# The denominators' matmuls join the visit in which keys meet values

## The chip, the cores and the metric

The kernel runs on one core of one Trainium2 chip. The metric is the time in microseconds (us) of one execution on the device. A core has a TensorE for matmuls (PE in the profile, its weight loads PEld), VectorE (DVE), ScalarE (ACT), GpSimdE (POOL), and SyncE (SP), which here only issues transfers. Matmuls write into PSUM, which has eight banks of 512 float32 columns on 128 partitions.

## The reference: linear attention, then a feed-forward layer

```python
proj = x @ w_phi                                   # per head, 64 -> 128
proj = proj - max(abs(proj), axis=-1)
phi(x) = concat([exp(proj), exp(-proj)])           # 256 features
kv  = einsum('bhsf,bhsd->bhfd', phi(k), v)
z   = sum(phi(k), axis=2)
num = einsum('bhsf,bhfd->bhsd', phi(q), kv)
den = einsum('bhsf,bhf->bhs', phi(q), z) + 1e-06
x   = (num / den) as [4608 tokens, 512]
h = x @ w_in;  e = exp(h - max(h));  solu = h * e / sum(e)
out = layernorm(solu) * g_ln @ w_out               # 512 -> 1024 -> 512
```

There are 8 batches with 8 heads of 576 tokens and 64 columns each. The 64 heads are worked through as 32 pairs of heads, and the feed-forward layer as 36 tiles of 128 tokens.

## The kernel before, in words

**Units and pairs.** A unit `u` (0 to 15) is one half of a batch: two pairs of heads, `sub` 0 and 1. Pair `n = 2u + sub`. For keys, a token tile of 256 or 128 columns is loaded (`rawk`), split into a high and a low part (`xh` on ACT, `xl` on POOL), projected (`pjk` on PE), reduced to its largest magnitude (`m`, DVE), shifted (`dk`, DVE) and put through exp twice (`ek`, ACT). Queries go `rawq`, `hq` (ACT, then POOL), `pq` (PE, four pieces of 288 tokens), `blk` (DVE transposes), a maximum over the features that passes PE twice (`mtp`, `mcp`) with DVE, POOL and ACT between, POOL subtracts, DVE transposes back (`pT`) and ACT makes the features `fq`. The first three units use other, plainer paths (`pjq`, `dT`).

**The visit.** For each pair, one function `visit` holds the PE in a tiled mode: the array is used as two halves of 64 columns, or as four strips of 32 columns, and several small matmuls run side by side. From pair 6 on (`JOIN`) the visit of pair n first makes the numerators of pair n-1 (`num`, two banks of 288 tokens, 64-column halves), then keys times values of pair n (`kvT`, 64-column halves), then the sums over the keys (`kvT<-zacc`, 32-column strips), in columns 256 to 383 of the same bank.

**The denominators.** `q_den` makes those of pair n-1: for two halves of 288 tokens, four matmuls on four 32-column strips, each half into a bank of its own (`den`). It is an operation of its own in the order: it may stand right behind the visit, or anywhere after it. ACT copies each half out (`dE`, `q_oe`). SP stores the rows to DRAM, loads them compactly (`cmp`), DVE takes the reciprocal (`cmr`), SP stores and broadcasts it (`rb`), and POOL multiplies it into the numerators (`xa`, `xb`).

**Keys-values on their way to the next visit.** DVE transposes the 384 columns of the visit's bank (`kvs`, `kv_turn`), SP stores them (`dk`), and four loads of 32 partitions each bring them back in the layout that the next visit's `num` and `den` take as weights (`kvf<-dk`, `kv_in`). Every SP transfer uses one of eight semaphores in turn.

**The feed-forward tile.** `h` (24 matmuls of 512 columns), maximum on DVE (`nm`), exp on ACT and product on DVE (`eu`), eight transposes on PE (`uT`), split on ACT and DVE (`uh`, `ul`), `o` (24 matmuls of 512 columns), scaling on ACT (`os`), store.

**PSUM.** Three banks are shared by all attention tiles (tag `a`: `pjk`, `pq`, `mtp`, `mcp`, `num`, `den`), one is the visit's alone (tag `kv`), `h` takes two, and two serve `uT` and `o` (tag `mo`).

**What sets the order.** `Plan.order` places every operation: it keeps a cost for each, latencies between engines, and a count of free buffers per tag; an operation is placed when its inputs and all its buffers are there, and among the ready ones priority decides. The priorities are the sums of two tables of numbers, `BASE` and `OFFSET`. The result is one fixed instruction order on each engine. At run time an engine works through its order and waits on semaphores at single instructions, so that a tile's bank is waited for at its first write, and not earlier.

```python
TILED = dict(visit=(1, 2), q_num=(1, 1), q_den=(2, 2))
PSUM_BUFS = dict(a=3, kv=1, h=1, mo=2)
```

Of the kernel before, what the change touches and what calls it, by code (L numbers as in the profile page):

```python
# [20 lines left out]
P = 128  # L21
KCOL = 2 * S
HC = S // 2
# [3 lines left out]
TILED = dict(visit=(1, 2), q_num=(1, 1), q_den=(2, 2))  # L27
K_PLAIN = (0, 1, 2)
# [19 lines left out]
PSUM_BUFS = dict(a=3, kv=1, h=1, mo=2)  # L48
# [19 lines left out]
)  # L68
OFFSET = (
# [289 lines left out]
def linear_attention_then_moe(ctx: ExitStack, tc, qT, qT2, kT, v, w_phi, w_in, g_ln, w_out, out):  # L359
# [22 lines left out]
    def bank(tag, shape, name):  # L382
        pool = psa if tag in ("a", "kv", "th", "tmo") else ps
        return pool.tile(shape, F32, tag=place(tag), bufs=1, name=name)
# [266 lines left out]
    def visit(st, sub, before):  # L651

        if before:
            q_num(*before)
        kv = st["kv", sub] = bank("kv", [P, 512], "kvT")
        for g in PARTS[sub]:
            e = st["kf", g]
            rv = st["rv", g] if g != 2 else st["vz"][:, sub : sub + 1]
# [645 lines left out]
```

## Time and profile before

| | |
|---|---|
| three runs | median 790.03 us (788.88 to 792.82) |
| the profiled execution's own time | 790.95 us |
| its span, first to last instruction | 789.2 us |
| mean granted TensorE clock | 0.994 |
| PE busy | 756.7 us |
| POOL, DVE, ACT busy | 470.9, 486.4, 405.8 us |

The profile is read as follows. A row of a group of instructions gives how often it ran, its busy time, the mean time of one in ns, and behind the second bar the idle time of its engine just before, with what ended it. A row of the timeline gives the start in us, the length, the engine, and what was made. A float32 matmul of this program is shown as two MATMUL instructions, a float32r one as one. The length of a matmul in the timeline is longer than its place in the stream, since matmuls overlap: the place is read from start to start.

### The profile page before, as it was taken

How to read it: one execution, taken by the hardware profiler on the slowest of the kernel's cores; microseconds unless marked ns; L12 is line 12 of the kernel's file. 1: busy time of each engine (PE TensorE's matmuls, PEld its weight loads, DVE VectorE, ACT ScalarE, POOL GpSimd, SP SyncE). 2: the span in 40 equal slices, each digit the busy share in tenths (PEclk: the TensorE clock that was granted, in tenths of full speed). 3: DMA queues.
4: the chain of work that ended last, by engine and by line, in shares of the span. 5: the costliest groups of instructions: out<-in, count | busy, mean ns of one | idle time of the engine just before them, and what ended most of it. 6: DMA issues, size and time to landing. Idle time of an engine off the chain costs nothing.

```text
span 789.2 us, 13661 instructions
## 1 busy us (share of the span) xinstructions
PE 756.7 (96%) x4935; PEld 562.2 (71%) x4935; DVE 486.4 (62%) x829; ACT 405.8 (51%) x814; POOL 470.9 (60%) x507
## 2 busy tenths in 40 slices
PE   5899898999999999999999999999999999999997
PEld 3565586767677777767776777777777776788886
DVE  4978684756675675756566686665756683444343
ACT  3876764564645565454745465463644655322322
POOL 1224897778687678585676759675776855231210
PEclk8999999999999999999999999999999999999999
DMA  6954442443526153442435343333334212200000
GB/s 203 374 122 122 104 103 52 108 110 104 119 73 135 53 123 104 106 100 70 125 81 121 85 108 100 90 88 92 87 99 114 78 43 78 52 28 14 27 28 27
DMA packets 105251, 75.96 MB, mean 96 GB/s; under 512 B 65376, under 2 KB 91488, under 8 KB 104672
## 3 DMA queue, kind: packets, MB, share of 16 engines
q1 hardware_dynamic: 105184, 75.10, 35.9%
q8 instruction: 39, 0.64, 0.4%
q14 instruction: 28, 0.23, 0.1%
HBM read 59.67 MB, written 15.38 MB: 95 GB/s over the span
## 4 chain that ended last, share of the span: by engine, by line
PE 72%; DMA 10%; DVE 5%; ACT 3%; POOL 3%; issue 3%; SPq 3%; ACTq 0%; POOLq 0%; DVEq 0%
PE o L347 21%; PE h L347 20%; PE kvT L347 9%; PE num L347 6%; PE pjk L347 5%; PE uT L347 3%; PE pq L347 3%; DMA rawq<-in_q 3%; PE den L347 3%; SPq L347 3%; DMA cmp<-d 2%; POOL hq L347 2%; DMA dk<-kvs 1%; PE pjq L347 1%; DMA rawk<-in_k 1%
## 5 line engine op out<-in xcount | busy, mean ns | idle before, releaser
L347 PE MATMUL o<-w_out_h,uh 128*128 128x512 f32 x288 | 116.0, 403 | 0.4 <-ACT uh L347 0.4
L347 ACT ACTIVATE ek<-dk 128x512 f32<-128x512 f32 (+1 forms) x160 | 87.2, 584 | 53.6 <-DVE dk L347 49.7
L347 PE MATMUL o<-w_out_h,ul 128*128 128x512 f32 x288 | 114.2, 397 | 0.0
L347 PE MATMUL o<-w_out_l,uh 128*128 128x512 f32 x288 | 113.9, 396 | 0.0
L347 POOL TENSOR_TENSOR zacc<-zacc,ek 128x512 f32<-128x512 f32 (+1 forms) x78 | 100.7, 1290 | 12.8 <-ACT ek L347 8.1
L347 POOL TENSOR_TENSOR hq<-rawq,hq 64x1152 fp32r<-64x1152 f32 x26 | 69.5, 2674 | 47.7 <-ACT hq L347 43.9
L347 PE MATMUL h<-win_h,mxh 128*128 128x512 f32 x288 | 93.6, 406 | 1.0 <-DVE eu L347 1.0
L347 PE MATMUL h<-win_h,mxl 128*128 128x512 f32 x288 | 90.8, 396 | 0.0
L347 PE MATMUL h<-win_l,mxh 128*128 128x512 f32 x288 | 90.6, 396 | 0.0
L347 DVE TENSOR_TENSOR ul<-uT,uh 128x512 fp32r<-128x512 f32 x72 | 48.2, 679 | 54.0 <-ACT uh L347 54.0
L347 ACT ACTIVATE fq<-pT 128x576 f32<-128x576 f32 x104 | 68.6, 688 | 17.3 <-DVE pT L347 14.0
L347 ACT CAST uh<-uT 128x512 fp32r<-128x512 f32 x72 | 41.6, 590 | 61.9 <-PE uT L347 48.8
L347 PE MATMUL num<-fq,kvf 128*64 128x288 f32 x512 | 69.2, 412 | 2.8 <-ACT win_h L347 1.8
L347 ACT ACTIVATE eu<-h,nm 128x1024 f32<-128x1024 f32 x36 | 40.3, 1118 | 57.6 <-DVE nm L347 57.5
L347 DVE TENSOR_REDUCE nm<-h 128x1 f32<-128x1024 f32 x36 | 43.8, 1218 | 41.7 <-PE h L347 41.6
L347 POOL TENSOR_TENSOR blk<-blk,mcol 128x1152 f32<-128x1152 f32 x26 | 55.6, 2137 | 17.2 <-ACT mcol L347 17.1
L347 PE MATMUL kvT<-ek,rawv 128*64 128x256 f32 x512 | 65.3, 387 | 0.0
L347 DVE STREAM_TRANSPOSE blk<-pq 128x288 f32<-128x288 f32 x104 | 46.5, 460 | 28.4 <-PE pq L347 22.8
L347 DVE TENSOR_TENSOR eu<-h,eu 128x1024 f32<-128x1024 f32 x36 | 43.9, 1220 | 32.4 <-ACT eu L347 32.4
L347 PEld LDWEIGHTS o<-w_out_h,ul 128*128 128x128 f32 x288 | 54.2, 188 | 13.6 <-DVE ul L347 0.4
L347 PEld LDWEIGHTS h<-win_h,mxl 128*128 128x128 f32 x288 | 54.2, 189 | 13.1 <-POOL mxl L347 0.2
L347 PEld LDWEIGHTS h<-win_l,mxh 128*128 128x128 f32 x288 | 54.1, 188 | 13.1
(107 smaller groups left out, 1584.1 us busy)
## 6 DMA issues: line engine op xcount, KB each, us to landing
rawq<-in_q SPq DMA_DIRECT2D x52, 288.0 KB
rb<-d SPq DMA_DIRECT2D x64, 144.0 KB
out<-os SPq DMA_DIRECT2D x36, 256.0 KB
rawk<-in_k SPq DMA_DIRECT2D x64, 128.0 KB
rawv<-in_v SPq DMA_DIRECT2D x64, 128.0 KB
dk<-kvs SPq DMA_DIRECT2D x28, 192.0 KB
kvf<-dk SPq DMA_DIRECT2D x112, 48.0 KB
wraw<-in_w_in SPq DMA_DIRECT2D x4, 1024.0 KB
```

The lines of the kernel that those rows point to most:

```text
L347: return self.tc.keep_in_program_order(method(*args, **kwargs))
```

## The change

The denominators of pair n-1 become part of the visit of pair n, for pairs 6 to 31. A new function, `q_den_joined`, is called at the visit's end, behind the sums over the keys. It splits the 576 tokens into 288, 224 and 64 (`DEN`): the first two share one bank of 512 columns, the last 64 tokens go to columns 384 to 447 of the visit's own bank. The copies follow (`den_oe`): one of 512 columns, one of 64 columns. `q_den` stays for the pairs that are not joined. The visit's bank comes from the shared group now, which has four banks; the operation `V` takes all four (two numerators, keys-values, denominators) when it is placed. The planner lets the transposition `kve` start before the denominators' part of the visit has ended. The two priority tables are replaced throughout.

```diff
+DEN = (288, 224, 64)
...
-PSUM_BUFS = dict(a=3, kv=1, h=1, mo=2)
+PSUM_BUFS = dict(a=4, h=1, mo=2)
...
-    -200.2, -1092.1, -271.3, 82.4, 164.5, 214.3, 259.1, 297.6, 340.8, 386.9, 433.6, 479.2, 529.5, 576.1, 626.1,
...
+    -465.0, -1432.2, -565.0, -22.2, 124.8, 203.9, 251.6, 298.6, 351.4, 395.4, 441.9, 492.3, 543.1, 595.6, 646.1,
...
-        kv = st["kv", sub] = bank("kv", [P, 512], "kvT")
+        kv = st["kv", sub] = bank("a", [P, 512], "kvT")
...
+        if before:
+            q_den_joined(*before, kv)
...
+    def q_den_joined(st, sub, kv):
+
+        po = st["den", sub, 0] = bank("a", [P, 512], "den")
+        st["den", sub, 1] = kv
+        for i, (out, c, c0) in enumerate(
+            ((po[:, :HC], 0, 0), (po[:, HC:512], 1, 0), (kv[:, 3 * F : 3 * F + D], 1, 512 - HC))
+        ):
+            n = DEN[i]
+            for s in range(2):
+                for j in range(2):
+                    r = slice(32 * (2 * s + j), 32 * (2 * s + j) + 32)
+                    nc.tensor.matmul(
+                        out[r], lhsT=st["kvf", sub][:, 2, r], rhs=st["qf", sub, c][:, j, s, c0 : c0 + n],
+                        start=i < 2, stop=True, skip_group_check=True,
+                    )
+
+    def den_oe(st, sub, c):
+
+        if c == 0:
+            st["dens", sub] = sb("dE", [P, S], name="dE")
+            nc.scalar.copy(out=st["dens", sub][:, :512], in_=st["den", sub, 0])
+        else:
+            nc.scalar.copy(out=st["dens", sub][:, 512:], in_=st["den", sub, 1][:, 3 * F : 3 * F + D])
...
-                alloc += [("a", ("abs", (pu, "num", ps_, c))) for c in range(2)]
-                early = {(pu, "qv", ps_, c, "num"): cost + (1 - c) * 2 * mm32(HC) for c in range(2)}
-                cost += 4 * mm32(HC)
+                num = [("a", ("abs", (pu, "num", ps_, c))) for c in range(2)]
+                alloc = num + alloc + [("a", ("abs", (pu, "den", ps_, 0)))]
+                den = sum(mm32(n) for n in DEN)
+                early = {(pu, "qv", ps_, c, "num"): den + cost + (1 - c) * 2 * mm32(HC) for c in range(2)}
+                early[u, "kve", sub] = den
+                cost += 4 * mm32(HC) + den
```

On PE, in the middle of the program before, a pair's denominators stand alone between feed-forward matmuls (`o`) and the next pair's query projections (`pq`); at the end of the name stands the size of what one matmul writes.

```order
L347 MATMUL o<-w_out_h,ul 128x512
L347 MATMUL den<-fq,kvf 32x288 x8
L347 MATMUL pq<-hq,w_hh 128x288
L347 MATMUL pq<-hq,w_l_84 128x288
L347 MATMUL pq<-hq,w_hh 128x288
L347 MATMUL pq<-hq,w_l_84 128x288
L347 MATMUL o<-w_out_h,uh 128x512
```

The pair's visit lies further up there, and the eight tiled matmuls of `den` have whole-array matmuls on both sides.

On PE of the changed program, one visit in the middle, with what stands ahead of it and behind it.

```order
L349 MATMUL o<-w_out_h,ul 128x512
L349 MATMUL num<-fq,kvf 64x288 x8
L349 MATMUL kvT<-ek,rawv 64x256 x8
L349 MATMUL kvT<-ek,vz_94 64x256 x2
L349 MATMUL kvT<-zacc,ones 32x128 x4
L349 MATMUL den<-fq,kvf 32x288 x4
L349 MATMUL den<-fq,kvf 32x224 x4
L349 MATMUL kvT<-fq,kvf 32x64 x4
L349 MATMUL uT<-ident,eu 128x128 x4
L349 MATMUL mtp<-ident,m_5107 36x128
L349 MATMUL pjk<-wph_h,xh 128x256
```

Numerators, keys-values, key sums and denominators are now one stretch. Counted over the whole program, PE enters a tiled stretch 53 times before and 38 times now. Of the denominators of the 26 joined pairs, 15 stood alone before and 11 stood right behind a visit.

On ACT of the changed program, the copies behind such a visit, with the semaphores on which each waits (PE_49, DVE_49, Pool_49 are those of the engines, DMAHW those of transfers).

```order
L349 COPY E<-num 128x288 [waits PE_49]
L349 CAST mxh<-xa 128x512
L349 COPY E<-num 128x288 [waits PE_49]
L349 COPY dE<-den 128x512 [waits DMAHW6_49,PE_49]
L349 ACTIVATE fq<-pT 128x2x288 [waits DVE_49,PE_49]
L349 ACTIVATE fq<-pT 128x2x288
L349 CAST xh<-rawk 128x128 [waits DMAHW5_49,PE_49,Pool_49]
L349 COPY dE<-kvT 128x64 [waits DVE_49]
```

The second copy of the denominators, of 64 columns, waits for DVE, and what DVE has to have done is the transposition of the same bank (`kvs<-kvT`). This holds in 22 of the 26 joined visits; in the other four, the transposition waits for the copy. The transposition waits for the last of the denominators' matmuls into its bank.

On SP of the changed program, the transfers behind one visit in the middle.

```order
L349 DMA dk<-kvs 128x384
L349 DMA vz_92<-in_v 64x128 x2
L349 DMA rawv<-in_v 128x256
L349 DMA d_4922<-dE 4x576
L349 DMA rawv<-in_v 128x256
L349 DMA kvf<-dk 32x12x32 x3
L349 DMA cmp<-d_4922 128x2x9
L349 DMA rawk<-in_k 128x128
L349 DMA rawk<-in_k 128x256
L349 DMA rawq<-in_q 64x1152 x2
L349 DMA kvf<-dk 32x12x32
L349 DMA rawq<-in_q 64x1152 x2
```

The fourth load of `kvf` stands behind the next pair's key and query loads; in the program before, the four loads stand together in 25 of 28 cases, and now in 15 of 28.

More of the change, by code (lines that the diff above doesn't have):

```diff
@@ L382, in bank @@
     def bank(tag, shape, name):
-        pool = psa if tag in ("a", "kv", "th", "tmo") else ps
+        pool = psa if tag in ("a", "th", "tmo") else ps
         return pool.tile(shape, F32, tag=place(tag), bufs=1, name=name)
@@ L1001, in linear_attention_then_moe @@
             tiles = [("e", g) for g in PARTS[sub]] + [("rv", g) for g in PARTS[sub]]
-            alloc, early = [("kv", ("kv", sub))], {}
+            alloc, early = [("a", ("kv", sub))], {}
             if u not in Z_PE:
@@ L1094, in linear_attention_then_moe @@
             joined = JOIN <= n + 1 < 4 * B
-            source = {"num": ("abs", ((n + 1) // 2, "V", (n + 1) % 2)) if joined else ("qo", sub), "den": ("qd", sub)}
+            visitor = ("abs", ((n + 1) // 2, "V", (n + 1) % 2))
+            source = {"num": visitor if joined else ("qo", sub), "den": visitor if joined else ("qd", sub)}
             if not joined:
@@ L1099, in linear_attention_then_moe @@
                     {(u, "qv", sub, 0, "num"): 2 * mm32(HC)})
-            add(("qd", sub), "tensor", 2 * mm32(HC), z + 5.5, q_den, (sub,), feat + [source["num"]],
-                [("a", ("den", sub, c)) for c in range(2)], fk, {(u, "qv", sub, 0, "den"): mm32(HC)})
+                add(("qd", sub), "tensor", 2 * mm32(HC), z + 5.5, q_den, (sub,), feat + [source["num"]],
+                    [("a", ("den", sub, c)) for c in range(2)], fk, {(u, "qv", sub, 0, "den"): mm32(HC)})
             for c in range(2):
                 for k, t in (("num", "E"), ("den", "dE")):
-                    add(("qv", sub, c, k), "scalar", act(HC, True), z + 5.1 + c, q_oe, (sub, c, k),
+                    own = (k, sub, c)
+                    fn, args, cols = q_oe, (sub, c, k), HC
+                    if joined and k == "den":
+                        fn, args, cols = den_oe, (sub, c), (512, D)[c]
+                        own = ("abs", ((n + 1) // 2, "kv", (n + 1) % 2)) if c else own
+                    add(("qv", sub, c, k), "scalar", act(cols, True), z + 5.1 + c, fn, args,
                         [source[k]] + ([("qv", sub, 0, k)] if c else []),
-                        () if c else [(t, (t, sub))], [(k, sub, c), (t, sub)])
+                        () if c else [(t, (t, sub))], [own, (t, sub)])
             add(("dr", sub), "sync", dma(16 * S), z + 6.4, den_rows, (sub,),
```

105 rows, old and new, of tables (BASE, OFFSET) are left out of this document.

## The prediction

> **What bounds the kernel now.** I read the page first: span, busy time by engine, granted clock.
>
> ```profile
> span 789.2 us, 13661 instructions
> PE 756.7 (96%) x4935; PEld 562.2 (71%) x4935; DVE 486.4 (62%) x829; ACT 405.8 (51%) x814; POOL 470.9 (60%) x507
> PEclk8999999999999999999999999999999999999999
> ```
>
> PE is busy for 756.7 of 789.2 us at the full clock; the next engine has 486.4. The windows view divides this into the start, the middle with the pairs of heads, and the end where only feed-forward tiles are left. Its columns are window, length, busy time and instructions of PE, PEld, DVE, ACT and POOL, granted clock, DMA share, GB/s.
>
> ```profile
> 0.00:100.00 100.00, 83.64 (x720) 55.57 (x721) 71.97 (x106) 66.27 (x139) 39.40 (x38) 0.95 0.61 183
> 100.00:680.00 580.00, 568.07 (x3727) 422.52 (x3729) 368.67 (x660) 309.75 (x625) 410.50 (x424) 1.00 0.38 94
> 680.00:789.20 109.20, 104.95 (x496) 84.13 (x488) 45.77 (x64) 29.79 (x52) 21.01 (x46) 1.00 0.08 27
> ```
>
> In the 580 us in which the joined pairs run, PE is idle for 11.9 us. So two things can be won there: matmul stream time, and those idle microseconds. The view of PE's waits in that window names them (us in total, times, longest).
>
> ```profile
> PE uT L347 <- DVE eu L347: 2.1, 1, 2.1
> PE pjk L347 <- ACT dE L347: 2.1, 2, 1.6
> PE mtp L347 <- DVE m L347: 1.4, 1, 1.4
> PE pq L347 <- DVE dk L347: 1.3, 1, 1.3
> PE h L347 <- DVE eu L347: 1.0, 1, 1.0
> PE num L347 <- DMA kvf<-dk: 0.9, 1, 0.9
> PE pq L347 <- POOL hq L347: 0.5, 1, 0.5
> PE den L347 <- ACT E L347: 0.5, 1, 0.5
> ```
>
> These eight are 9.8 us. No wait recurs at every pair: each is a single place where the order was tight.
>
> **The change part by part.** *A: fewer tiled stretches.* What a stretch of denominators costs alone and behind a visit is read from start to start in the timeline of PE (start, length, what). First a place with whole-array matmuls only, then one with denominators between such matmuls.
>
> ```profile
> 303.19 0.39 PE L347 MATMUL o<-w_out_h,ul 128*128 128x512 f32 x1
> ...
> 303.55 0.29 PE L347 MATMUL pq<-hq,w_l 128*128 128x288 f32 x1
> ...
> 328.66 0.39 PE L347 MATMUL o<-w_out_h,ul 128*128 128x512 f32 x1
> 328.99 1.18 PE L347 MATMUL den<-fq,kvf 128*32 128x288 f32 x16
> ...
> 330.33 0.29 PE L347 MATMUL pq<-hq,w_l 128*128 128x288 f32 x1
> ```
>
> From the `o` row to the second `pq` row it is 0.36 us without and 1.67 us with denominators: 1.31 us alone. Then the end of a visit, without and with denominators behind the key sums.
>
> ```profile
> 361.61 0.42 PE L347 MATMUL kvT<-zacc,ones 128*32 128x128 f32 x8
> ...
> 362.09 0.60 PE L347 MATMUL uT<-ident,eu 128*128 128x128 f32 x4
> 389.28 0.43 PE L347 MATMUL kvT<-zacc,ones 128*32 128x128 f32 x8
> ...
> 390.73 0.60 PE L347 MATMUL uT<-ident,eu 128*128 128x128 f32 x4
> ```
>
> From the key sums to `uT`: 0.48 and 1.45 us, so 0.97 us joined. A pair that moves saves 1.31 − 0.97 = 0.34 us. By the order, 15 of the 26 pairs stood alone; the other 11 already stand behind their visit and save nothing. **A = −15 × 0.34 = −5.1 us.** Bounds: if what is paid around a lone stretch is paid elsewhere, 0; if all 26 gained, −8.8.
>
> *B: three groups in place of two.* The columns stay 576. Joined, 288 columns take 0.97/2 = 0.49 us, so 64 take 0.11 us. What the third group adds is weight loads, shown by the tile's own row (shortest, median, longest in ns).
>
> ```profile
> L347 PEld LDWEIGHTS den<-fq,kvf x512: 106/110/110, 34.1 to 680.3; 128*32 128x32 f32 x171
> ```
>
> A load is 0.110 us, and each strip of the third group has two (`j` 0 and 1) with little streaming to hide under. Both fully hidden cost nothing more; both in full view cost 0.22 us where 0.11 us of columns were paid, so +0.11. I take +0.08 a pair, nearer the upper end, because a group this short hides less than a long one. **B = 26 × 0.08 = +2.1 us**, bounds 0 to +2.9. The Trainium skill ("TensorE: Matmul & The Clock Gate", LDWEIGHTS) puts a weight load at its columns over 1.2 in ns, an estimate of 27 ns for 32 columns; by that B would be about 0 and the sum 2.1 us lower. The row's 110 ns does not agree with it, and decides.
>
> *C: banks and copies.* Four banks are shared where three were, and one pair's denominators take one of them and not two. These rows price what holds a bank.
>
> ```profile
> L347 ACT COPY dE<-den 128x288 f32<-128x288 f32 x64 | 25.3, 401 | 13.1 <-PE den L347 12.2
> L347 ACT COPY mcol<-mcp 128x36 f32<-128x36 f32 x26 | 4.8, 184 | 23.1 <-PE mcp L347 23.1
> L347 ACT CAST mxh<-xa 128x512 fp32r<-128x512 f32 x20 | 12.3, 619 | 1.7 <-DMA out<-os 1.6
> L347 ACT ACTIVATE fq<-pT 128x576 f32<-128x576 f32 x104 | 68.6, 688 | 17.3 <-DVE pT L347 14.0 <-PE kvT L347 3.3
> L347 DVE STREAM_TRANSPOSE kvs<-kvT 128x384 f32<-128x384 f32 x28 | 16.0, 570 | 39.5 <-PE kvT L347 39.2
> ```
>
> ACT's two copies were 2 × 0.40 us. Now they have 512 and 64 columns: near 0.6 us (the cast of 512) and, between the 36 columns' 0.18 and the 288's 0.40, 0.21 us. That is the same ACT time, and ACT is at 51%. The waits on ACT go: `pjk` behind `dE`, 2.1 us, and `den` behind `E`, 0.5 us. Matmuls between two places of the order are priced by pitches from start to start (0.235 us for 512 columns, in E's rows). So counted, the bank that the first two groups fill next comes back to a matmul at least 1.5 us of matmuls later; it needs the 0.6 us copy and two handovers, so it is covered. The visit's own bank needs more: last denominators, `kvs` on DVE (0.57), the 64-column copy (0.21), three handovers, and its next writer is about 5 us of matmuls away in most pairs (1.9 us in one). **C = −2.6 us.** Bounds: −2.6, and upwards a new wait at every pair if a `fq` (0.69 us) runs ahead of the copies: 0.6 + 0.69 + handovers of about 0.4 is 1.7 against the 1.5, so 26 × 0.2 = +5.2. What queues behind the 64-column copy on ACT while it waits for DVE is `fq` and `uh`, on which the next visit and `o` depend; in its row `fq` waits 14.0 us in all for DVE and none for ACT's own order. The Trainium skill ("PSUM — Partial Sum Buffer", Terms) says that two engines on one bank and quadrant at once collide, reads included; that fits copy and transposition taking turns, and no run here shows a collision.
>
> *D: the new order elsewhere.* The priorities are all new, so each wait of the list above may go and others come. Two were traced through the new order. `uT` behind `eu`, 2.1 us: it arose where 2.9 us of matmuls lay between the last `h` and `uT`, so 5.0 us were needed; now at least 5.5 lie there. `mtp` behind `m`, 1.4 us: less than 3.3 us of matmuls lay between `pq` and `mtp` in 10 of 26 pairs, now in one. **D = −3.5 us.** Bounds: all other waits of the list too except those of C, −7.2; or as many new ones of the same size as the two removed, about +4.
>
> *E: keys-values on their way.* The transposition waits for the last denominators' matmul into its bank, so this path starts 0.97 us later in the 26 pairs, whatever the planner lets start early. The chain of waits shows it where it decides, at the last pair (start, length, what), with one query load and the pitch of `h` from the timeline.
>
> ```profile
> 667.49 2.56 PE kvT L347 x28
> 670.07 0.59 DVE kvs L347
> 670.68 1.85 DMA dk<-kvs
> ...
> 674.58 0.57 SPq L347
> ...
> 675.19 2.30 DMA kvf<-dk
> ...
> 677.63 2.16 PE num L347 x16
> ```
>
> ```profile
> 672.40 0.63 PE L347 MATMUL h<-win_h,mxh 128*128 128x512 f32 x2
> 672.87 0.63 PE L347 MATMUL h<-win_l,mxh 128*128 128x512 f32 x2
> 160.64 5.46 DMA rawq<-in_q
> ```
>
> The path takes 677.63 − 670.05 = 7.58 us; 6.7 us of matmuls covered it and 0.9 us was waited. Now the denominators stand ahead of its start, and 24 matmuls of `h` at 0.47/2 us and the change of mode, 5.9 us, remain: 1.7 us waited, **+0.8 us**. At the other pairs a median of 16 us of matmuls covers the path. But the fourth `kvf` load has moved behind query loads in nine pairs, and in four of these it stands so late in the joint order of all engines that 0.3 to 0.4 us of matmuls are left before `num`. SP runs ahead of that order when its waits are met, so it mostly goes out earlier; I take one SP issue (0.6 us) lost at each of the four, **+2.4 us, E = +3.2 us**. Bounds: +0.8, and each of the four waiting for its whole transfer, 2.30 + 0.14 − 0.35 = 2.1 us, so +9.2.
>
> *The start and the end.* Before pair 6 nothing is joined. By the order 66 us of matmuls stand ahead of the first `h`, 73 before, but PE is idle for 16.4 us of the first 100, and its DMA share of 0.61 there is the highest of the three: the loads bound it and have not moved, so 0, bounds ±2. The last tiles repeat their pattern.
>
> **Sum:** −5.1 + 2.1 − 2.6 − 3.5 + 3.2 = −5.9 us, made against the span of 789.2 us: 783.3. The profiled execution took 790.95, 0.9 above the runs' median, so I carry the difference to the median: 790.03 − 5.9 = **784.1 us**.
>
> **The rivals.** *More falls away:* the four-bank group takes all the middle's listed waits but the one at the last pair (8.9 of 9.8) and the late loads go out early (E = 0.8): −5.1 + 2.1 − 8.9 + 0.8 = −11.1, about 779; with all 26 joined at the best price (A −8.8) 775.2. For it: no wait recurs, so a better order can remove each. Against it: an order this full makes new single waits.
>
> *The gain is swallowed:* the copies behind each visit are late by the 0.2 us of C's upper bound. −5.9 + 5.2 = −0.7, about **789.3**. For it: two copies, a transposition and `fq` now compete behind the same last matmul, where one bank could be emptied while the other was filled. Against it: ACT's share of 51%, and the 5 us before the visit's bank is written again. The Trainium skill ("TensorEngine Tiling (Array Packing)", PSUM Bottleneck) warns that tiling speeds up TensorE and not the emptying of PSUM; it would come out here as this rival, and before the change the 12.2 us in `dE`'s row are ACT waiting for PE, not the reverse.
>
> *Slower:* the fourth `kvf` load, behind two 288 KB query loads, is held until the first of these has landed: 5.46 − 2 × 0.6 = 4.2 us after its own issue. At the four places that is 4.2 + 0.14 − 0.35 = 4.0 us each, 16.0, and at the five others, with some 3 us or more left, up to 1.3 us each. With the four alone, −5.9 − 2.4 + 16.0 = +7.7: **797.7 us**. It decides once these loads cost above 2.4 + 5.9 = 8.3 us, 2.1 us at each of the four. For it: their place in the order; the one wait for `kvf` seen was real. Against it: SP has slack, and its order is not a timetable.
>
> *Not what it says:* the planner's early start for the transposition has no counterpart in the order's waits; that is in E. The visit itself is joined in all 26, so this rival has no case of its own.
>
> **How the numbers follow.** The forecast 784.1 has a chance of 0.50, its own range 780 to 788; more falling away 0.13; swallowed 0.22; slower 0.15. A measurement of this kernel can tell about 0.5% from no change, that is 786.1 to 794.0. Faster: four fifths of the forecast (0.40), the 0.13 and little of the swallowed case (0.02): 0.55. Slower: most of the slower case (0.13) and a little of the swallowed one (0.02): 0.15. Same: 0.30. The range goes from 775.5, close to the best case, to 796, a little short of the slower one.
>
> **What the changed profile would show.** A and B: no `den` between whole-array matmuls in pairs 6 to 31, and about 0.97 + 0.08 = 1.05 us from the key sums to the next whole-array matmul beyond its 0.48; 1.3 or more there would undo A. C: no PE wait on `dE` above 0.3 us; a row of many small ones on `dE` or `kvs` is the swallowed case. D: `uT` behind `eu` and `mtp` behind `m` gone, and PE's idle time in the middle below 8 us. E: `num` behind `kvf` once, near 1.7 us; several of 2 us or more are the slower case. The forecast is wrong if the middle's PE idle time rises, or if PE's busy time does not fall by about 3 us.

## The result, and the profile after

The changed kernel took a median of 797.75 us (793.41 to 801.44, 6 runs) against 790.37 us (788.47 to 792.82, 6 runs): a ratio of 1.008 (95% interval 1.0053 to 1.0108), 7.4 us slower. 784.1 was forecast, with 775.5 to 796 as the range. In a second set of runs it was 797.41 against 788.21 us, a ratio of 1.0105 (1.0077 to 1.0133), 9.2 us slower; the experiments below stand beside that.

The page of the changed kernel, its first lines:

```profile
span 796.2 us, 14095 instructions
PE 755.3 (95%) x5143; PEld 573.8 (72%) x5143; DVE 490.6 (62%) x829; ACT 401.4 (50%) x814; POOL 471.0 (59%) x507
PEclk9999999999999999999999999999999999999999
```

PE is still the engine that fills the span, and its busy time fell by 1.4 us; yet the span is 7.0 us longer. So PE is idle for 40.9 us where it was 32.5. The windows view of the changed kernel, with the columns of before:

```profile
0.00:100.00 100.00, 78.72 (x634) 53.21 (x635) 76.63 (x111) 63.16 (x131) 40.91 (x41) 0.95 0.58 176
100.00:680.00 580.00, 566.76 (x3958) 435.48 (x3957) 370.05 (x655) 304.64 (x625) 404.71 (x420) 1.00 0.39 94
680.00:796.20 116.20, 109.77 (x555) 85.13 (x553) 43.94 (x65) 33.59 (x61) 25.41 (x48) 0.98 0.11 33
```

PE's idle time grew in all three stages: from 16.4 to 21.3 us in the start, from 11.9 to 13.2 in the middle, from 4.3 to 6.4 in the last, whose clock is also below 1. PE's waits between 100 and 680 us (us in total, times, longest):

```profile
PE pq L349 <- DVE mt L349: 3.8, 3, 1.8
PE num L349 <- DMA kvf<-dk: 2.0, 2, 1.4
PE num L349 <- DVE ul L349: 1.4, 1, 1.4
PE o L349 <- DVE ul L349: 1.1, 2, 0.8
...
PE pq L349 <- ACT dE L349: 0.9, 1, 0.9
...
PE pq L349 <- DVE kvs L349: 0.8, 1, 0.8
PE pjk L349 <- ACT E L349: 0.7, 1, 0.7
```

Twelve rows sum to 14.0 us, 11.1 before. The waits that the prediction wanted gone are nearly gone (`uT` behind `eu` 2.1 to 0.2, `mtp` behind `m` 1.4 to 0.4), and others stand in their place: 6.2 us of them (`mt` 3.8, `dE` 0.9, `kvs` 0.8, `E` 0.7) are for a bank.

**Where these come from** is seen on ACT. The rows of its casts of keys, before and after:

```profile
L347 ACT CAST xh<-rawk 128x256 fp32r<-128x256 f32 x52 | 20.4, 406 | 15.7 <-PE pjk L347 9.1 <-issue 3.8 <-DMA rawk<-in_k 2.3
```

```profile
L349 ACT CAST xh<-rawk 128x256 fp32r<-128x256 f32 x52 | 21.0, 405 | 51.0 <-DMA rawk<-in_k 30.5 <-PE pjk L349 10.4 <-issue 4.5
```

In these rows (the tiles of 256 columns) ACT waited 2.3 us for key loads, and now 30.5 us. One of these waits, followed through the engines in the timeline of the changed kernel (start, length, what; the idle time before it in brackets): first SP, then ACT, DVE and PE.

```profile
418.52 1.16 SPq L349 DMA_DIRECT2D rawq<-in_q  x2
419.72 0.60 SPq L349 DMA_DIRECT2D kvf<-dk  x1
420.37 1.26 SPq L349 DMA_DIRECT2D rawq<-in_q  x2
...
422.36 0.38 SPq L349 DMA_DIRECT2D rawk<-in_k  x1
428.08 0.40 ACT L349 CAST xh<-rawk 128x256 fp32r<-128x256 f32 x1 [6.40 <-DMA rawk<-in_k]
428.39 1.15 ACT L349 CAST hq<-rawq 128x1152 fp32r<-128x1152 f32 x1
429.45 1.11 ACT L349 ACTIVATE eu<-h,nm 128x1024 f32<-128x1024 f32 x1
430.68 1.23 DVE L349 TENSOR_TENSOR eu<-h,eu 128x1024 f32<-128x1024 f32 x1 [3.81 <-ACT eu L349]
432.75 0.84 DVE L349 STREAM_TRANSPOSE pT<-blk 128x288 f32<-128x288 f32 x2 [0.84 <-POOL hq L349]
433.51 1.24 DVE L349 BATCH_NORM_STATS2 bst<-eu 128x6 f32<-128x512 f32 x2
...
435.62 0.54 DVE L349 STREAM_TRANSPOSE kvs<-kvT 128x384 f32<-128x384 f32 x1
436.08 0.24 DVE L349 TENSOR_REDUCE mt<-mtp 36x32 f32<-36x128 f32 x1
436.38 0.40 PE L349 MATMUL pq<-hq,w_hh 128*128 128x288 f32 x1 [1.80 <-DVE mt L349]
```

A 128 KB key load was issued behind four query loads of 288 KB (and one `kvf` load) and used 5.7 us after its issue. ACT stood for 6.4 us, `eu` behind it came late, DVE waited 3.8 us for it, and so `kvs` and `mt`, behind that work in DVE's order, emptied their banks late. The visit ended at 431.76; its bank was given up at 436.2. PE, with all four shared banks taken, waited. That is the reading; the experiments test it.

**A second loss, the clock.** Windows of 3.4 us of the changed kernel, two pairs of neighbours (columns as above; the granted clock is third from the end):

```profile
180.10:183.50 3.40, 1.66 (x10) 1.07 (x8) 2.63 (x5) 1.84 (x4) 3.32 (x3) 1.00 0.38 55
183.50:186.90 3.40, 3.30 (x14) 1.91 (x16) 2.22 (x6) 1.02 (x2) 0.63 (x1) 0.50 0.41 143
692.10:695.50 3.40, 1.51 (x10) 0.92 (x10) 1.46 (x3) 0.11 (x1) 1.26 (x1) 1.00 0.30 40
695.50:698.90 3.40, 3.40 (x21) 1.58 (x21) 2.23 (x3) 1.79 (x4) 0.39 (x2) 0.50 0.32 87
```

In these pairs PE was busy for about half of a stretch, and the next ran at half clock. By an estimate from these rows, a wait of 1.4 to 2 us then costs about 1.7 us more: half of a busy stretch of 3.4 us. Half of PE's busy time in all stretches at half clock, from the trace, is 7.7 us after and 4.8 us before.

The account of the two profiled executions: tiled stretches −2.9 us (below), PE's waits of the middle without the last pair's +3.8 (10.2 to 14.0), the last pair's wait for `kvf` +1.0 (0.9 to 1.9), PE's waits ahead of 110 us +4.0 (16.9 to 20.9), half clock +2.9. That is 8.8 against 7.0 us; −1.8 us are left unattributed.

Without going by single waits, the span is PE's idle time and its busy time: idle time rose by 8.4 us, half clock by 2.9, and the busy time at full clock fell by 4.3, together 7.0. So matmul time was saved, more than the tiled stretches show, and idle time took it back. A second profile of the changed kernel, below, has +10.2, +1.9 and −5.6, together +6.5 us, with 24.7 us of waits ahead of 110 us in place of 20.9: what a single stage lost is known to a few us only.

### The profile page after: what moved, and what is told of

The parts are those of the page before. It is cut to its first block, busy times and chain, and to the rows that moved or that the text cites. A ratio compares the mean times of both kernels' runs of the same rounds, so it can differ in the third digit from the quotient of the medians.

```text
span 796.2 us, 14095 instructions
## 1 busy us (share of the span) xinstructions
PE 755.3 (95%) x5143; PEld 573.8 (72%) x5143; DVE 490.6 (62%) x829; ACT 401.4 (50%) x814; POOL 471.0 (59%) x507
## 4 chain that ended last, share of the span: by engine, by line
PE 68%; DMA 10%; DVE 8%; SPq 5%; ACT 4%; POOL 3%; issue 2%; POOLq 0%; ACTq 0%
PE o L349 21%; PE h L349 19%; PE kvT L349 8%; PE num L349 7%; SPq L349 5%; PE uT L349 3%; PE pjk L349 3%; PE den L349 3%; DVE w L349 2%; PE pq L349 2%; DMA rawk<-in_k 2%; DMA rawq<-in_q 2%; DMA kvf<-dk 2%; DMA wraw<-in_w_out 1%; DMA cmp<-d 1%
## 5 line engine op out<-in xcount | busy, mean ns | idle before, releaser
L349 ACT ACTIVATE fq<-pT 128x576 f32<-128x576 f32 x104 | 68.9, 685 | 20.8 <-DVE pT L349 19.0
L349 PE MATMUL num<-fq,kvf 128*64 128x288 f32 x512 | 72.1, 425 | 5.3 <-DMA kvf<-dk 3.9
L349 PEld LDWEIGHTS o<-w_out_h,uh 128*128 128x128 f32 x288 | 54.2, 188 | 14.2 <-DVE ul L349 1.7
L349 PEld LDWEIGHTS h<-win_l,mxh 128*128 128x128 f32 x288 | 54.1, 188 | 13.2
L349 PEld LDWEIGHTS o<-w_out_l,uh 128*128 128x128 f32 x288 | 54.3, 188 | 11.2
```

What stands on the lines that cost most here:

```text
L349: return self.tc.keep_in_program_order(method(*args, **kwargs))
```

## The experiments

Most edits keep the order on PE between the pairs 6 and 31: the one that takes the denominators out moves them there, those of the start touch only what lies ahead of pair 6, and the combined kernel only the last visit. So two kernels can be compared between two instructions that both have: the starts of the numerators of pair 6 and of pair 31, in the timelines of the profiled executions. The medians are of several executions; beside the first row the kernel before had 790.37 us, beside the next four 788.21, then 789.36 (four rows), 788.98 (two), 789.81 and 790.38. These groups ran on several chips, so across groups the ratios are to be compared and not the medians.

| kernel | median us (lowest to highest) | ratio to before, 95% | pair 6 at | pair 6 to pair 31 |
|---|---|---|---|---|
| changed, first profile | 797.75 (793.41 to 801.44) | 1.008 (1.0053 to 1.0108) | 145.9 | 548.9 |
| changed again | 797.41 (794.13 to 800.28) | 1.0105 (1.0077 to 1.0133) | 149.9 | 546.1 |
| queries behind keys | 788.40 (785.04 to 791.51) | 0.9992 (0.9971 to 1.0012) | 146.2 | 538.3 |
| kvs first on DVE | 800.50 (796.43 to 801.38) | 1.0137 (1.0111 to 1.0163) | 151.6 | 547.2 |
| first keys first | 795.27 (792.99 to 799.90) | 1.0083 (1.0056 to 1.0111) | 147.2 | 545.2 |
| kvf together | 801.32 (796.73 to 802.45) | 1.0157 (1.0123 to 1.0191) | 149.4 | 548.6 |
| denominators apart | 808.40 (807.87 to 810.02) | 1.0256 (1.0230 to 1.0282) | 150.4 | 554.5 |
| both SP edits | 788.92 (786.88 to 791.30) | 1.0000 (0.9979 to 1.0020) | 147.5 | 540.2 |
| combined | 786.42 (785.70 to 789.52) | 0.9975 (0.9956 to 0.9994) | 147.6 | 538.4 |
| start of 160 operations | 791.92 (786.13 to 795.87) | 1.0030 (1.0011 to 1.0050) | 152.2 | 541.6 |
| start of 369 operations | 797.94 (796.82 to 800.05) | 1.0115 (1.0100 to 1.0129) | 159.4 | 538.6 |
| filled | 788.60 (786.63 to 792.93) | 0.9991 (0.9972 to 1.0010) | 146.3 | 539.2 |
| start of 78 operations | 789.44 (787.52 to 793.03) | 1.0006 (0.9983 to 1.0030) | 148.6 | 542.4 |

The edits work on the planner's finished sequence: one engine's order is changed by the lines shown, and all other engines keep theirs; where the denominators are apart and in the starts, several engines' orders change. `put(line, a, b)` moves operation `a` right behind `b`, or to a position. In the names, `kl` is a key load, `ql` a query load, `wp` a half of the projection weights, `kve` the transposition `kvs`, `qmx` the reduction `mt`, `qb` the transposes `pT`, and `kvi` a load of `kvf`.

### The changed kernel again

> The changed kernel without any edit, beside the kernel before on one chip, so that the edits have a base of the same chip. Its profile so far has a span of 796.2 against 789.2 us. If the loss is in the order of the instructions, the same waits come back in about the same places (PE: pq behind mt 3.8 us in 3, num behind kvf 3.9 us in 3; ACT: xh behind the key loads 28 us in 8) and the time is again about 7 us (0.9%) above the kernel before. If the loss was a matter of that one execution, waits and places differ and the time lies within 3 us of the kernel before.

797.41 us, 9.2 above the kernel before. The same waits came back (`pq` behind `mt` 3.8 us in 3, `num` behind `kvf` 4.5 us in 3, `xh` behind key loads 23.0 us in 9). The loss is there a second time, with the same waits, so it is in the order. What moved by 4 us from one execution to the other is the start (pair 6 at 145.9 and 149.9).

### Two query loads behind the key load

```diff
+    def queries_behind(line):                   # SP
+        for u in (4, 5, 6, 7, 9, 10, 11):
+            put(line, (u + 1, "ql", 1, 0), (u, "kl", 4))
+            put(line, (u + 1, "ql", 1, 1), (u + 1, "ql", 1, 0))
```

> Changed kernel; only SP's order differs: in seven units (4, 5, 6, 7, 9, 10, 11) the two query loads of 288 KB that are wanted some 20 us later are issued behind the last key load of the unit, which is wanted 3 to 4 us later. Theory L (late key loads): ACT waits 28.0 us for key loads (2.3 us before the change), holds back eu, E and the exps behind it, so DVE transposes and reduces late and PE waits for a bank. Then ACT's wait falls to under 15 us, PE's waits for mt, kvs and dE (5.5 us in all) fall to under 2 us, and the time falls by 3 to 5 us against the changed kernel. Rival B (the four banks taken at once are the cause, whatever the loads do): ACT's wait falls but PE's bank waits stay at 4 us or more, and the time changes by less than 1.5 us.

788.40 us: 9.0 us less than the changed kernel on the same chip, twice what was expected, by moving 14 of 590 issues. The same pair's place in the timeline, SP and then ACT, and below it PE's waits for banks and for `kvf` between 100 and 680 us, and ACT's for key loads between 100 and 690:

```profile
412.64 0.51 SPq L349 DMA_DIRECT2D rawq<-in_q  x1
413.20 0.59 SPq L349 DMA_DIRECT2D kvf<-dk  x1
413.83 0.62 SPq L349 DMA_DIRECT2D rawq<-in_q  x1
...
415.18 0.38 SPq L349 DMA_DIRECT2D rawk<-in_k  x1
...
418.73 0.41 ACT L349 CAST xh<-rawk 128x256 fp32r<-128x256 f32 x1 [2.81 <-DMA rawk<-in_k]
```

```profile
PE pjk L349 <- ACT E L349: 1.1, 1, 1.1
...
PE pq L349 <- DVE mt L349: 0.8, 1, 0.8
PE num L349 <- DMA kvf<-dk: 0.7, 1, 0.7
PE pq L349 <- ACT dE L349: 0.6, 1, 0.6
...
ACT xh L349 <- DMA rawk<-in_k: 14.8, 7, 4.0
```

The key load is used 3.5 us after its issue, not 5.7; ACT's wait for key loads is 14.8 us, where the two profiles of the changed kernel have 28.0 and 23.0; PE's waits of the middle are 7.2 us, not 14.0 and 13.7, and those for a bank 2.5, not 6.2. Theory L holds, and rival B falls: with the four banks taken at once as before the edit, most of the bank waits went with the lateness of ACT. The gain is more than the 6.5 to 6.8 us of PE's waits. No half-clock stretch is left between 43 us and the end of this execution, where the two of the changed kernel had one or two behind pair 6, of about 1.7 us each; that can be the rest. The edit begins behind pair 6, so the start is not part of its gain.

### kvs and mt first on DVE

```diff
+    def kvs_first(line):                        # DVE
+        for n in (20, 22, 26):
+            u, sub = n // 2, n % 2
+            at = where(line, (u, "qb", 0, 0))
+            put(line, (u, "kve", sub), at)
+            put(line, (u, "qmx", 1), at + 1)
```

> Changed kernel; only DVE's order differs, at the three visits where PE waited 1.8, 1.2 and 0.8 us for a bank behind mt: the transposition kvs and the reduction mt stand ahead of the transposes pT and the statistics bst instead of behind them. If those banks are held by DVE's order behind late work, these three waits (3.8 us) go and the time falls by 2.5 to 4 us. If they are only where a lateness shows that the stream carries anyway (late loads, late ACT), PE waits as long at the next place (h, uT or pq behind eu, dk or blk) and the time changes by less than 1 us.

800.50 us, 3 us more than the changed kernel, with ranges that overlap. PE's largest wait of the middle is now this:

```profile
PE o L349 <- DVE ul L349: 5.2, 5, 2.2
```

Of the 3.8 us behind `mt` 0.6 are left, and 5.2 us stand behind `ul`, where the changed kernel had 2.5 (`o` 1.1 and `num` 1.4): in this order `ul` is the next thing that DVE does late. All of PE's waits of the middle are 13.8 us, as in the changed kernel (14.0 and 13.7). The bank wait was where the lateness showed, not what made it.

### The first key loads first

```diff
+    def keys_first(line):                       # SP
+        put(line, (0, "kl", 1), 0)
+        put(line, ("wp", 1), ("wp", 0))
+        put(line, (0, "kl", 0), ("wp", 1))
```

> Changed kernel; only the first SP issues differ: the two first key loads and both halves of the projection weights are issued ahead of the values and queries, as the first key load is in the kernel before. PE's first matmul starts at 7.05 us in the changed kernel and at 5.86 us before. If the start is bound by the first load, the first matmul starts 1.2 to 2.5 us earlier and the time falls by 1 to 2.5 us; if the start is bound by all loads together (share of the DMA engines 0.58 in the first 100 us), the next loads come as much later, PE's second wait (2.6 us for rawq) grows by as much, and the time changes by less than 0.5 us.

795.27 us, 2.1 less than the changed kernel beside it, by medians whose ranges overlap. PE's first matmul starts at 3.9 us (7.05 before the edit), but pair 6 comes at 147.2, as in the others: the 3 us are not kept. Together with the query edit it won nothing (788.92 against 788.40). So the first load alone does not bound the start.

### The four kvf loads together

```diff
+    def kvf_together(line):                     # SP
+        for n in range(JOIN, 4 * B - 1):
+            for i in range(1, 4):
+                put(line, (n // 2, "kvi", n % 2, i), (n // 2, "kvi", n % 2, i - 1))
```

> Changed kernel without the moved query loads; only SP's order differs: the four kvf loads of a pair stand together everywhere, so that no fourth load is behind query loads. Moving two query loads in seven units won about 9 us, and in four of these units it also put the fourth kvf load ahead of them. Theory L (late key loads are what counts): PE's waits for kvf in the middle (2.0 to 2.5 us) go, ACT still waits above 20 us for key loads, and the time falls by 0.5 to 2.5 us against the changed kernel (797.4). Rival K (the late kvf loads were it): the time falls by 5 us or more.

801.32 us, by the ratios 0.5% above the changed kernel, about 4 us; ACT still waits 28.6 us for key loads in 9. No wait for `kvf` is left in the middle, and PE's waits there are 14.3 us all the same. Rival K falls, and theory L's own small gain did not come either: other waits stand in place of those for `kvf`.

### The denominators taken out of the visit

```diff
-        if before:
-            q_den_joined(*before, kv)
...
+    for n in range(JOIN, 4 * B):
...
+        sequence[i + 1 : j + 1] = rest + [sequence[j], {**den, "engine": "tensor", "after": []}] + early
```

Here `i` is the visit's place, `j` that of the next operation on PE, and `early` holds the copies and the transposition that need the denominators. The banks are the same.

> The kernel with the two query loads behind the key load, and in addition the denominators (all three groups, same banks) taken out of the visit and put behind the next matmul operation on PE (four uT in most pairs, twelve h or o in others); nothing else moves but the copies and the transposition that need them. If joining saves a change of mode, as the stretches of the two profiles say (1.43 us alone less the 0.235 us of the matmul ahead, and 0.97 joined: 0.23 us a pair), the time rises by 26 x 0.23 = 6 us, and by up to 10 us where the later transposition holds the bank longer. If a change of mode is hidden, the time stays within 1.5 us of 788.4.

808.40 us, 20.0 more than its base, which is the kernel with the query loads behind (20.8 by the ratios), and twice the 10 us that were expected at most. One visit's end on PE, first in the base, then apart:

```profile
424.63 0.43 PE L349 MATMUL kvT<-zacc,ones 128*32 128x128 f32 x8
424.88 1.05 PE L349 MATMUL den<-fq,kvf 128*32 128x288 f32 x16
425.74 0.29 PE L349 MATMUL kvT<-fq,kvf 128*32 128x64 f32 x8
425.96 0.66 PE L349 MATMUL uT<-ident,eu 128*128 128x128 f32 x4
426.45 0.27 PE L349 MATMUL mtp<-ident,m 128*36 128x128 f32 x1
```

```profile
437.17 0.42 PE L349 MATMUL kvT<-zacc,ones 128*32 128x128 f32 x8
437.53 0.66 PE L349 MATMUL uT<-ident,eu 128*128 128x128 f32 x4
438.12 1.07 PE L349 MATMUL den<-fq,kvf 128*32 128x288 f32 x16
439.00 0.29 PE L349 MATMUL kvT<-fq,kvf 128*32 128x64 f32 x8
439.23 0.29 PE L349 MATMUL mtp<-ident,m 128*36 128x128 f32 x1
```

From the key sums to `mtp` it is 1.82 us joined and 2.06 us apart: 0.24 us a pair, 6.2 us for 26, as expected. The rest was not: PE's waits between 100 and 680 us are 11.0 us in place of 7.2 in the base, the wait for `kvf` at the last pair rose from 1.8 to 4.6 us, and half the busy time at half clock from 3.5 to 9.6 us. In an order made for the joined visit, taking it apart costs three times the matmul time that joining saves; that shows what the join is worth in this order, not against the kernel before, whose order is another.

### Both SP edits, and the last visit turned round

> The two edits of SP's order together: query loads behind the key load, and the first key loads first. If the gains are independent (9.0 and 2.1 us against the changed kernel), 786 to 787 us, which is 1 to 2 us faster than the kernel before (788.2); if the start is made good later anyway, 788 us.

788.92 us, the time of the kernel before beside it: the gains are not independent.

```diff
+        last = (st["u"], sub) == (2 * B - 1, 1)
-        if before:
+        if before and not last:
             q_num(*before)
...
+        if last:
+            q_den_joined(*before, kv, (2,))
+            q_num(*before)
+            q_den_joined(*before, kv, (0, 1))
```

> The same two edits, and in the last joined visit (pair 31) another order of the matmuls: keys times values, key sums and the 64-token group of the denominators first, then the numerators and the other two groups. The transposition of keys-values then starts about 2.9 us earlier (numerators 2.0 us and the two groups 0.9 us are behind it and not ahead). If PE's wait of 1.8 to 2.0 us for kvf at the last pair is that path and nothing else, it goes, and the time falls by 1.8 us against the two edits alone (784.5 to 785.5), and by up to 1.7 us more in executions in which the wait was followed by a window of half clock. If something else is late there (E or the exps on ACT), the wait changes its name and the time stays.

786.42 us, 2.5 less than the two edits alone. The wait for `kvf` at the last pair fell from 1.9 to 1.1 us, not to nothing, so it explains at most a third of that difference:

```profile
PE num L349 <- DMA kvf<-dk: 1.1, 1, 1.1
```

This is the one kernel of the study that beats the kernel before, by 0.25% (0.06 to 0.44%). It is one of twelve comparisons, measured on one chip and not repeated, so a gain this small is not settled.

### The start in the order of before

```diff
+START_ORDER = [
...
+    def start_as_before():
+        rank = {n: i - len(START_ORDER) for i, n in enumerate(START_ORDER)}
...
```

The list holds the first 160, 369 or 78 operations in the order of the kernel before. They come first, then the combined kernel's order without its edit of the first loads; buffers are given out anew in that sequence.

> The combined kernel (786.4 us) without its edit of the first loads; instead the first 160 operations, on all engines, stand in the order in which the kernel before has them (about the first 40 us); all later ones keep the combined kernel's order. In the first 100 us PE is busy for 79 us in it and for 83.6 us in the kernel before, and the mean clock of its runs is 0.991 against 0.996. If the rest of the lost time lies in the order of the start, the first matmul comes at 5.9 us, PE's waits ahead of 100 us fall by 2 to 4 us, the mean clock rises to 0.993 or more, and the time falls by 2 to 5 us, to 781 to 784.5. If the loads bound the start in either order, it stays within 1 us of 786.4.

> As the kernel before this one, with the first 369 operations (about the first 80 us) in the order of the kernel before the change. If the loss is spread over the whole start, this wins 1 to 3 us more than the first 160 operations alone; if it is in the first loads and matmuls, the two agree within 1 us. Where the two orders meet, a buffer may be wanted by both, and that could cost 1 to 2 us there (a new wait on PE between 80 and 110 us).

> The combined kernel (786.4 us) with only the first 78 operations (about the first 22 us) in the order of the kernel before the change. The same with 160 operations made PE busy for 27.9 us of the first 40 (24.8 in the combined kernel, 28.4 before), but lost it again in waits of 3.2 us at 47 and at 63 us, where the two orders meet. If the loss of the start lies in the first loads and matmuls and the meeting place is quiet this time, PE's waits ahead of 110 us fall from about 18 to 15 us or less and the time falls by 1 to 3 us; if each start is only good as a whole, new waits stand between 20 and 60 us and the time is 787 us or more.

791.92, 797.94 and 789.44 us, all above the combined kernel. PE's waits ahead of 110 us are 24.3, 32.1 and 24.7 us, against 21.3 there. The largest of them, of the start of 369 operations, stands where the orders meet:

```profile
PE pq L721 <- POOL hq L721: 9.2, 1, 9.2
```

With 160 operations PE was busy for 27.9 of the first 40 us, and then waited 3.2 us twice. These three don't say what the start of the changed kernel costs; they say only that none of these starts could be put in front of this order without new waits. What the start costs stays open.

### Idle matmuls in the start

```diff
+        (0, "qp", 2): ("mo0", 13), (1, "qp", 0): ("a0", 9), (3, "qp", 0, 1): ("a0", 6), (3, "qp", 0, 2): ("a0", 2),
...
+        for i in range(count):
+            nc.tensor.matmul(idle[:, :P], lhsT=ident, rhs=ident, start=True, stop=True)
```

> The combined kernel (786.4 us) with matmuls that compute nothing (identity on identity into a bank that is free then, 30 in all, 0.22 us each at full clock) at four places of the start where PE stands idle in all profiles of this family: 13 at the wait for the queries at 13.5 us (3.1 us), 9 at the wait for dk at 34.6 us (2.0 us), 6 and 2 at the waits at 86 and 88 us (1.2 and 0.4 us). Theory W (a stretch of 3.4 us in which PE was busy for about half is followed by one at half clock, and that is where part of the loss of this family lies): the half-clock stretches at 14.5 to 21, 38 to 45 and 90 to 93 us, which cost 6.9 us of matmul time in the combined profile, mostly go, the mean clock rises from 0.990 to 0.995 or more, and the time falls by 2 to 5 us (781.5 to 784.5). Rival: what follows those stretches is bound by loads and by DVE in any case, so the clock rises and the time stays within 1 us; or the clock does not follow PE's idle time at all, and the added matmuls cost up to 1 us.

788.60 us: the ratio to the kernel before is 0.9991, against 0.9975 without. The same two stretches, first without, then with idle matmuls:

```profile
35.00:40.00 5.00, 2.27 (x11) 1.57 (x12) 5.00 (x8) 5.00 (x11) 2.36 (x1) 0.84 0.77 270
40.00:45.00 5.00, 5.00 (x42) 2.83 (x44) 5.00 (x8) 2.86 (x4) 0.84 (x1) 0.50 0.18 54
```

```profile
35.00:40.00 5.00, 4.35 (x33) 3.41 (x30) 5.00 (x8) 5.00 (x11) 2.38 (x1) 1.00 0.77 258
40.00:45.00 5.00, 4.96 (x81) 3.15 (x77) 5.00 (x8) 3.84 (x7) 0.67 (x1) 1.00 0.36 99
```

The clock follows PE's busy time: with the pause filled, the half-clock stretch at 38 to 45 us is gone, and so is the one at 90 us; of the first one, at 14 us, half is left. Of 12 executions the mean clock was 0.994, and 0.990 without. The time did not follow: the first matmul of `h` came at 100.0 us in place of 101.1, and pair 6 at 146.3 in place of 147.6, but part was paid again by a fill that waited 2.5 us for a bank. So the rival holds for these places: half clock in the start costs little. That what follows there is bound by loads, DVE and ACT is the likely reason and was not tried. That half clock costs its 1.7 us in the middle, where PE is the bound, was not tried by itself.

## Why the prediction was wrong

By its terms: C and D together were given −6.1 us, and PE's waits of the middle, without those for `kvf`, rose by 1.8 (10.2 to 12.0); the start was given 0 and its waits rose by 4.0; half clock was given nothing and took 2.9 us more of PE's busy time. A, B and E came out near their sums. Both signs of being wrong that the prediction named came: the middle's idle time rose, and PE's busy time fell by 1.4 us and not by about 3.

**A, fewer tiled stretches (−5.1): right in kind, too large.** All tiled stretches of the trace, from the start of the matmul ahead to the first whole-array matmul: a lone one has a median of 1.43 us, a visit 4.93, a joined visit 5.90 before. A lone one holds the matmul ahead too (0.235 us), so joining saves 1.43 − 0.235 − (5.90 − 4.93) = 0.23 us, and not 0.34, which came from one place. 15 × 0.23 = 3.4 us.

**B, the third group (+2.1): wrong, it is free.** The joined visit with three groups has a median of 5.91 us, with two 5.90. The added weight loads are as long as the row said (0.110 us), but they are loaded under the columns ahead. By the rule of the Trainium skill ("TensorE: Matmul & The Clock Gate", LDWEIGHTS) B came out near 0. The trace agrees with that sum and not with its 27 ns a load. A and B together were given −3.0; from the sums of all joined pairs' stretches, without waits and half clock, they are −2.9 us. That the two agree is luck: one error was too much saved, the other too much paid.

**C, banks (−2.6): the step that failed, through its cover.** The waits named did go (`pjk` behind `dE`, `den` behind `E`, 2.6 us), but 6.2 us of bank waits came. The cover was counted as matmul time between a bank's last and next use, with DVE and ACT free to empty it at once. At the visit shown above, the bank was emptied 4 us late, behind a late load. The +3.6 us net lie within the bound of +5.2, by another mechanism than the `fq` named there.

**D, the order elsewhere (−3.5): both named waits went (3.5 to 0.6), and others of 2.5 us behind `ul` came.** The bound named such new ones; the value taken did not.

**What C and D missed is one thing.** SP's order was read for `kvf` and for what stands behind the visit, but not for when each key load is issued against its use. Matched one by one in the two traces, from the issue on SP to the cast on ACT, the last key load of each of the units 4 to 13 was issued 25 to 38 us ahead of its cast before, and is issued 2.2 to 9.0 us ahead now, behind up to four query loads: in most of these units ACT stands until the load lands. In seven of these units (4 to 7 and 9 to 11) query loads that are wanted later stood ahead, and the edit moved those. The query edit puts these loads two query loads further ahead in the queue. At the pair shown the key load is then issued 2.5 us behind the first query load and not 3.8, and in the seven units the median from issue to cast is 3.7 us and not 5.0. That took ACT's wait from 28.0 and 23.0 to 14.8 us, and it took back 9.0 of the 9.2 us. The prediction's row on `kvf` (E) had the right queue and the wrong load: it asked what the query loads delay, and did not ask it of the load that ACT waits for.

**E (+3.2): about right.** PE's waits for `kvf` are 3.9 us after and 0.9 before, so +3.0: 1.9 us at the last pair (1.7 forecast) and 2.0 us in the middle (2.4). The measured time is the slower rival's (797.7), but not by its mechanism, so that match is luck: its 16 us behind `kvf` were 2.0, and putting the loads together made the time no shorter.

**The start (0 ± 2): wrong.** PE's waits ahead of 110 us rose by 4.0 us, by 7.8 in the second profile, and by 5.3 in the kernel with the query edit. That the loads bound the start and had not moved was argued from the DMA share; their order had moved: the first key load is the fifth issue, and PE begins 1.2 us later. Putting it first did not win the time back, so which part of the new start costs is open.

**The clock was left out.** "Full clock" was read from tenths of 40 slices, in which a stretch of 3.4 us does not show.

With the loads mended, the time is that of the kernel before and not 5.9 us less, though PE's waits of the middle are 7.2 us where they were 10.2. By the waits, the start takes back most of it (22.2 us, 16.9 before) and the last pair about 1 us. The one profile of this kernel was a fast execution (786.03 us, against 790.95 for that of the kernel before), so this is an account by waits and not of the medians. How much of the start belongs to this order was not settled.

## What to carry to other kernels

When a new order moves loads, list for every load how long ahead of its use it is issued and how many bytes stand ahead of it in its queue; an engine that works in order stops at the one late load, and the wait shows three engines further on. A bank's cover is only as good as the lateness of the engine that empties it: before blaming a bank, look at what the emptying engine was waiting for. And a gain in matmul time of 0.4% (2.9 us) is smaller than what seven late loads cost here (9.0 us).

## What the runs showed of the hardware

Two things were not expected. Weight loads of 0.110 us for a group that streams 64 columns cost nothing in the stream of tiled matmuls. And the clock drops to half for stretches of 3.41 us, or two or four times that, after a stretch in which PE was busy for too little of it. Counted over all 14 profiles in such windows: of those at full clock, all 26 in which PE was busy for less than about 1.4 us were followed by one at half clock, none of the 3050 with more than about 2.0 us was, and 20 of the 50 between. Where such a pause was filled with idle matmuls, the drop was gone. The Trainium skill ("TensorE: Matmul & The Clock Gate", Part 1) describes a free-running window of 3413 ns and half rate after an idle one. The traces agree on the length, but here a window that was busy for 40% was already too little. The window's place against the kernel differs from execution to execution, so one wait falls into one window in one and across two in the next: between the first 25 and the last 2 us, the half-clock stretches of two executions of the changed kernel stood at 88, 184 and 696 us, and at 39, 66 and 438 us.
